# Early keys in fp32 on the SyncE queue with a ScalarE cast, a halved output copy, and new engine orders, in a fused attention and expert kernel

## The chip, the cores and the metric

The kernel runs on one NeuronCore of one Trainium2 chip. The metric is the device time of one execution in microseconds (us); smaller is better. A trace also gives the span from the first to the last instruction, about 1.8 us shorter than that time. Engines: PE (TensorE matmuls), PEld (its weight loads), ACT (ScalarE), DVE (VectorE), POOL (GpSimd), SP (SyncE, which only issues DMAs here). "Granted clock" is TensorE's share of full speed.

Most executions of one kernel agree within a per cent; now and then one takes 2 to 3% longer, as one of the first three of the kernel before did (175.25 us). Those count as slow and are left out of every ratio and median below.

## The reference

Shortened and rewritten. Eight batches, eight heads, 576 positions, head width 64. Keys and values are averaged over groups of eight positions, attention runs on the 72 pooled keys, and its output `x` (8 x 576 x 512) goes through four attention experts with causal masks, of which two are picked for each position.

```python
def reference(q, k, v, w_gate, wq, wk, wv, wo):        # shortened
    k_p = k.reshape(B, H, 72, 8, 64).mean(axis=3)       # pooling
    v_p = v.reshape(B, H, 72, 8, 64).mean(axis=3)
    attn = softmax(q @ k_p.T / 8.0)
    x = (attn @ v_p).transpose(0, 2, 1, 3).reshape(B, 576, 512)
    logits = x @ w_gate                                 # 4 experts, top 2, weights by softmax
    for e in range(4):
        a = softmax(causal(x @ wq[e] @ (x @ wk[e]).T / 8.0))
        out += gate[e] * (a @ (x @ wv[e]) @ wo[e])
    return out                                          # 8 x 576 x 512, fp32
```

## The kernel before

One long list of tokens gives PE, ACT, DVE and POOL their orders. A token is a step, its batch after the colon, its PSUM bank after `@`, and a final `d` if DVE, not ACT, does the copy. Each engine runs its own steps strictly in the list's order. POOL issues the loads and also applies the causal masks.

```python
def load(b, nm, c):          # L_q, L_k, L_v: fp32 in HBM, bf16 in SBUF: the DMA casts on its way
    if nm == "q":
        dst = qraws[b % NRAW][:, c, :, :]
        ...
    nc.gpsimd.dma_start(out=dst, in_=src)

def warm_up(n, bank):        # Hn: n matmuls on nothing, to bring the clock up and keep it up
    for _ in range(n):
        nc.tensor.matmul(out=psum[:, bank, :], lhsT=warm[:, 0:128], rhs=warm[:], start=True, stop=True)

def am(b, ep, ti):           # a00 ... a12: causal mask on POOL, after ACT's exp of the same scores
    ...
            nc.gpsimd.affine_select(out=blk, in_=blk, ...)

def y(b, bank, dve, c):      # last step of a tile: copy out of PSUM, then DMA to HBM on SyncE
    ofin = ofp.tile([128, DM], FP32, name="ofin", tag="ofin")     # 8 buffers in turn
    copy(dve, ofin[:], psum[:, bank, :])
    if c == 4:
        for h in range(2):   # two half tiles, two DMAs
            nc.sync.dma_start(out=out[b - 1 + h, MAIN:S, :], in_=ofin[64 * h : 64 * h + 64, :])
    else:
        nc.sync.dma_start(out=out[b, 128 * c : 128 * c + 128, :], in_=ofin[:])

SEQ = """ I:0 L_k0:0 L_k1:0 L_k2:0 J:0 L_q0:0 K:0 L_q1:0 L_q2:0 L_q3:0 L_q4:0 L_q5:0 H19:0@0
          PK:0@0 L_v0:0 kc:0d L_v1:0 H3:0@1 KT:0@0 ...
          ... Y4:7@5 y1:7 Y2:7@6 y2:7d y4:7d """
```

`PK` pools the keys, `KT` and `Q` transpose keys and queries, `E` are the first scores, `P` the expert projections, `S`, `B`, `T`, `Y` the expert scores, values, transposes and output.

The softmax here doesn't subtract the row's maximum and nothing guards it: scores larger than these inputs give would overflow.

Of the kernel before, what the change touches and what calls it, by code (L numbers as in the profile page):

```python
# [8 lines left out]
FP32 = mybir.dt.float32  # L9
# [12 lines left out]
def kernel(  # L22
# [33 lines left out]
    KR = 96  # L56
# [52 lines left out]
    def load(b, nm, c):  # L109
        if nm == "q":  # L110
            dst = qraws[b % NRAW][:, c, :, :]
            src = q[b, :, KR * c : KR * (c + 1), :].rearrange("h p d -> p h d")
        else:
            raw, T = (kraws, k) if nm == "k" else (vraws, v)
            dst = raw[b % NRAW][:, c, :, :, :].rearrange("p h t d -> p h (t d)")
            src = T[b, :, 2 * KR * c : 2 * KR * (c + 1), :].rearrange("h (p t) d -> p h (t d)", t=2)
        nc.gpsimd.dma_start(out=dst, in_=src)  # L117

# [376 lines left out]
    def y(b, bank, dve, c):  # L495
        ofin = ofp.tile([128, DM], FP32, name="ofin", tag="ofin")
        copy(dve, ofin[:], psum[:, bank, :])
        if c == 4:
            for h in range(2):
                nc.sync.dma_start(out=out[b - 1 + h, MAIN:S, :], in_=ofin[64 * h : 64 * h + 64, :])  # L500
        else:
            nc.sync.dma_start(out=out[b, 128 * c : 128 * c + 128, :], in_=ofin[:])
# [7 lines left out]
        I:0 L_k0:0 L_k1:0 L_k2:0 J:0 L_q0:0 K:0 L_q1:0 L_q2:0 L_q3:0 L_q4:0 L_q5:0 H19:0@0  # L510
        PK:0@0 L_v0:0 kc:0d L_v1:0 H3:0@1 KT:0@0 L_v2:0 kt:0 L_k0:1 L_k1:1 H8:0@1 Q0:0@0 Q2:0@1
        r0:0 Q3:0@2 L_k2:1 Q1:0@3 r3:0d E0:0@4 r1:0 r2:0d L_q0:1 E3:0@6 M:0 e0:0 E4:0@2 E2:0@0
        L_q1:1 e3:0 E1:0@4 L_q2:1 e1:0 L_q3:1 PV:0@6 L_q4:1 vc:0d e4:0 H1:0@7 D0:0@4 e2:0 L_q5:1
        H1:0@5 D2:0@5 O01:0@6 O00:0@7 d0:0 W1:0 H1:0@2 O11:0@0 O10:0@1 x0:0 O20:0@2 D1:0@4 d2:0
        d1:0 o00:0 W0:0 H1:0@3 PK:1@3 o01:0 kc:1 W3:0 x1:0 H3:0@5 KT:1@3 W2:0 kt:1 o11:0 x2:0
        o10:0 L_v0:1 L_v1:1 H9:0@4 Q1:1@3 Q0:1@1 L_v2:1 r1:1d Q2:1@0 r0:1 Q3:1@6 L_k0:2 E1:1@4
        r3:1d c2:0 c3:0d H1:0@3 E0:1@6 L_k1:2 e1:1 r2:1d P_k0:0@3 o20:0 E3:1@4 L_k2:2 p_k0:0
        E4:1@0 P_k1:0@2 c0:0 L_q0:2 c1:0 P_q0:0@3 e4:1 c4:0d L_q1:2 e3:1 P_q1:0@0 p_k1:0d e0:1
        V2:0@1 p_q0:0d L_q2:2 V0:0@2 p_q1:0d E2:1@4 S00:0@6 v0:0d e2:1 V1:0@3 L_q3:2 v2:0d
        P_t0:0@2 v1:0d s00:0 D1:1@4 PV:1@3 L_q4:2 d1:1 V3:0@5 vc:1d a00:0 D0:1@6 x1:1 v3:0d  # L520
        L_q5:2 O10:1@3 d0:1 O11:1@4 o10:1 D2:1@5 S10:0@0 p_t0:0 O01:1@6 x0:1 o11:1 L_v0:2
        O00:1@7 S02:0@2 s10:0 o01:1 PK:2@4 L_v1:2 o00:1 d2:1 x2:1 S01:0@0 s02:0 g1:0 L_v2:2
        V3:1@5 kc:2d P_q0:1@7 g2:0 L_k0:3 s01:0 v3:1d g3:0 g4:0 L_k1:3 Q1:2@6 p_q0:1 Q0:2@0
        r1:2d KT:2@1 g0:0 L_k2:3 V1:1@5 r0:2d Q2:2@4 kt:2d L_q0:3 Q3:2@0 v1:1d r2:2 V2:1@1 r3:2d
        E0:2@6 L_q1:3 g5:0 v2:1 E2:2@4 E3:2@2 e0:2 P_k0:1@1 L_q2:3 e3:2 a02:0 P_q1:1@0 p_k0:1d
        L_q3:3 e2:2 E1:2@2 p_q1:1d S03:0@6 PV:2@1 a10:0 e1:2 L_q4:3 O20:1@4 D1:2@0 o20:1 V0:1@5
        vc:2d d1:2 L_q5:3 P_t0:1@4 s03:0 v0:1d V4:1@2 L_v0:3 x1:2 p_t0:1d D0:2@3 g6:0 O01:2@5
        L_v1:3 d0:2 O00:2@4 O11:2@6 PK:3@7 x0:2 o11:2 W4:0 O10:2@3 S02:1@0 v4:1 o01:2 P_k1:1@6
        kc:3 L_v2:3 o00:2 g0:1 s02:1 L_k0:4 KT:3@7 o10:2 Q3:3@5 Q0:3@4 L_k1:4 r3:3 Q1:3@2 g1:1
        Q2:3@3 g2:1 r0:3d r1:3 V2:2@0 a01:0 kt:3d P_q0:2@1 p_k1:1 g3:1 L_k2:4 g4:1 r2:3d g5:1  # L530
        v2:2d S12:0@6 a03:0 p_q0:2 S11:0@2 g6:1 L_q0:4 g7:0 S00:1@4 g8:0 s12:0 V3:2@0 g9:0
        L_q1:4 P_k1:2@1 v3:2d s11:0 g7:1 L_q2:4 g8:1 B00:0@0 s00:1 V1:2@6 a11:0 bz00:0 bg00:0
        P_k0:2@7 a12:0 b00:0 p_k1:2 v1:2d L_q3:4 E4:2@4 p_k0:2d E1:3@2 e4:2 E2:3@0 V0:2@6 a00:1
        g9:1 e2:3 L_q4:4 B10:0@7 v0:2d B11:0@4 bz10:0 L_q5:4 e1:3 bg10:0 D2:2@6 PV:3@5 bz11:0
        bg11:0 L_v0:4 S01:1@0 d2:2 vc:3d S10:1@2 x2:2 B01:0@6 s01:1 L_v1:4 b10:0 P_q1:2@5 bz01:0
        L_v2:4 s10:1 bg01:0 b01:0 E3:3@0 b11:0 L_k0:5 S12:1@6 p_q1:2d e3:3 S11:1@2 PK:4@4 a01:1
        g1:2 a02:1 T1:0@5 s12:1 kc:4d T0:0@0 Q1:4@1 L_k1:5 t1:0d D1:3@4 s11:1 r1:4d E0:3@6
        L_k2:5 t0:0d O20:2@5 Q0:4@1 e0:3 o20:2 Y0:0@0 L_q0:5 r0:4d Q2:4@5 g2:2 E4:3@2 d1:3
        L_q1:5 r2:4d S03:1@6 Y3:0@1 e4:3 y0:0d P_t0:2@5 L_q2:5 s03:1 y3:0d D0:3@4 x1:3 D2:3@6
        O11:3@7 a11:1 p_t0:2d O10:3@0 d2:3 O01:3@1 d0:3 o11:3 a12:1 O00:3@6 O20:3@5 S02:2@2 x0:3  # L540
        o10:3 a03:1 KT:4@7 s02:2 a10:1 B01:1@4 o00:3 L_q3:5 B00:1@0 bz01:1 g3:2 kt:4 B10:1@6
        o01:3 L_q4:5 x2:3 B11:1@2 g0:2 bz00:1 bg01:1 bz10:1 Q3:4@1 o20:3 L_q5:5 P_k0:3@7 bz11:1
        r3:4d bg11:1 L_v0:5 bg00:1 bg10:1 b00:1 P_k1:3@5 p_k0:3 b01:1 L_v1:5 b11:1 P_q1:3@7
        p_k1:3 b10:1 L_v2:5 E2:4@4 p_q1:3d L_k0:6 S00:2@0 e2:4 S01:2@2 V0:3@6 g4:2 L_k1:6 V2:3@7
        s00:2 v0:3d V3:3@4 L_k2:6 v2:3d V1:3@5 s01:2 L_q0:6 V4:3@0 v1:3d Q1:5@1 v3:3 v4:3d
        L_q1:6 E3:4@6 S10:2@2 g1:3 e3:4 T0:1@0 r1:5d a01:2 Q2:5@4 t0:1d a00:2 P_q0:3@5 s10:2
        g5:2 L_q2:6 r2:5d g6:2 g2:3 Q3:5@0 p_q0:3d a02:2 E1:4@6 E4:4@2 PK:5@1 e1:4 g3:3 r3:5d
        L_q3:6 PV:4@5 g4:3 g7:2 g8:2 D1:4@0 e4:4 L_q4:6 vc:4d B00:2@6 d1:4 S03:2@2 g9:2 L_q5:6
        bz00:2 E0:4@4 kc:5d s03:2 Y2:0@7 e0:4 L_v0:6 bg00:2 P_t0:3@2 y2:0d T1:1@3 x1:4 L_v1:6
        KT:5@1 b00:2 D0:4@0 g0:3 D2:4@7 t1:1d O00:4@4 d0:4 a03:2 O11:4@6 kt:5d O20:4@5 L_v2:6  # L550
        O10:4@3 g5:3 p_t0:3 O01:4@1 g6:3 x0:4 o10:4 PV:5@0 L_k0:7 Y1:0@2 o11:4 vc:5 Y4:1@3
        L_k1:7 d2:4 o00:4 B01:2@0 x2:4 y1:0 o20:4 a10:2 S12:2@6 y4:1 o01:4 L_k2:7 S11:2@4
        P_t0:4@2 s12:2 g7:3 bz01:2 g8:3 L_q0:7 P_q0:4@1 g9:3 bg01:2 s11:2 b01:2 L_q1:7 p_t0:4d
        Q0:5@6 Y3:1@0 p_q0:4d r0:5 a12:2 V2:4@4 y3:1d S10:3@2 a11:2 S00:3@6 v2:4d s10:3 S02:3@0
        L_q2:7 V0:4@5 V3:4@4 L_q3:7 s02:3 v0:4d Q0:6@2 P_k0:4@3 L_q4:7 r0:6d s00:3 v3:4d L_q5:7
        B10:2@2 E3:5@0 p_k0:4 bz10:2 E2:5@6 L_v0:7 bg10:2 e3:5 E0:5@4 b10:2 B11:2@3 a00:3 Y2:1@2
        e2:5 L_v1:7 bz11:2 bg11:2 V1:4@0 y2:1d P_q1:4@1 a02:3 e0:5 b11:2 v1:4d a10:3 E4:5@2
        E1:5@6 p_q1:4d e4:5 S01:3@4 Y0:1@0 e1:5 T1:2@1 y0:1d T0:2@2 P_k1:4@3 s01:3 t1:2d t0:2d
        S03:3@0 S12:3@6 p_k1:4d a01:3 s03:3 S11:3@4 Q3:6@2 s11:3 Y0:2@3 Y3:2@0 y0:2d s12:3
        D0:5@1 a11:3 D1:5@4 y3:2d PK:6@3 d0:5 O20:5@5 g1:4 a12:3 D2:5@6 O10:5@7 kc:6d d2:5  # L560
        O00:5@0 d1:5 O11:5@1 a03:3 r3:6d O01:5@6 x2:5 Y1:1@3 L_v2:7 x1:5 o20:5 Q1:6@2 B10:3@4
        o11:5 r1:6 V4:5@5 o10:5 x0:5 B11:3@2 y1:1 bz10:3 Y2:2@1 o00:5 v4:5 Q2:6@7 bg10:3 KT:6@3
        g0:4 bz11:3 y2:2 o01:5 B01:3@0 B00:3@5 kt:6 r2:6d Q3:7@1 bz01:3 V3:5@3 bg01:3 bz00:3
        g2:4 r3:7 b01:3 V0:5@7 bg11:3 bg00:3 b10:3 Q0:7@6 v0:5 V2:5@1 b11:3 v3:5 P_q0:5@4 r0:7d
        v2:5d b00:3 T1:3@6 p_q0:5 V1:5@7 t1:3d S01:4@2 g3:4 v1:5d E3:6@4 s01:4 S02:4@0 g1:5
        P_k0:5@7 g4:4 g2:5 g3:5 s02:4 a01:4 T0:3@6 p_k0:5d P_k1:5@2 e3:6 a02:4 g4:5 t0:3d
        S00:4@0 p_k1:5d E2:6@6 g0:5 s00:4 E0:6@4 Y3:3@3 P_q1:5@2 e2:6 y3:3d a00:4 S10:4@0 e0:6
        p_q1:5d E1:6@6 PV:6@3 g5:5 g5:4 g6:5 s10:4 g6:4 D1:6@2 vc:6d Y1:2@4 Q2:7@5 g7:4 d1:6
        y1:2d Y1:3@3 a10:4 e1:6 P_t0:5@0 r2:7d PK:7@2 y1:3d x1:6 S03:4@4 g7:5 g8:4 D0:6@1 kc:7d
        s03:4 O10:6@3 O01:6@6 d0:6 a03:4 o10:6 O00:6@7 O11:6@2 p_t0:5 S11:4@4 x0:6 o11:6 S12:4@0  # L570
        B01:4@3 s11:4 o00:6 Y0:3@2 o01:6 s12:4 B00:4@7 a11:4 Q1:7@4 g9:4 g8:5 bz00:4 V1:6@6
        r1:7d y0:3 a12:4 S00:5@0 bg00:4 v1:6 b00:4 E4:6@4 V2:6@2 s00:5 g9:5 bz01:4 KT:7@7
        P_q1:6@6 v2:6d e4:6 kt:7d a00:5 bg01:4 S12:5@0 b01:4 E3:7@4 p_q1:6d S02:5@2 e3:7 B11:4@7
        P_q0:6@6 bz11:4 s02:5 bg11:4 b11:4 B10:4@4 p_q0:6d s12:5 V0:6@5 a02:5 bz10:4 V3:6@2
# [80 lines left out]
```

## Time and profile before

| kernel before | |
|---|---|
| time, three runs | 170.39, 170.50, 175.25 us (the last slow) |
| span of the profiled run, granted clock | 168.5 us, 1.000 |
| PE busy, of it warm-ups | 156.5 us, 12.8 us (45) |
| start of the last part of the first pooling, of the first scores, of the first projection | 8.38, 13.22, 25.60 us |
| last matmul, last landing, end of the span | 162.96, 167.61, 168.53 us |

The profile's page of the kernel before, busy time and the chain of waits (the chain that ended last, followed back):

```profile
PE 156.5 (93%) x2075; PEld 91.5 (54%) x2103; DVE 123.3 (73%) x395; ACT 135.2 (80%) x240; POOL 105.7 (63%) x178
...
PE 66%; ACT 10%; POOL 10%; DMA 4%; DVE 4%; issue 3%; DVEq 1%; POOLq 0%
```

PE bounds the kernel; only its idle times, its warm-ups and the two ends are to be had. The timeline of PE at the start (start, duration, engine, line, what; in brackets the idle time before and what ended it):

```profile
1.26 5.96 PE L172 MATMUL psum<-warm 128*128 128x512 bf16 x19 [1.26 <-DVE onesd L146]
...
8.38 0.59 PE L178 MATMUL psum<-kraw_71,poolk 96*32 96x512 bf16 x4 [0.85 <-DMA kraw_71<-in_k_dram]
...
12.27 0.98 PE L182 MATMUL psum<-ident,qraw_68 96*128 96x96 bf16 x19 [0.23 <-DMA qraw_68<-in_q_dram]
13.22 0.42 PE L178 MATMUL psum<-qT_83,kpT_79 64*96 64x512 bf16 x2
...
25.60 0.81 PE L178 MATMUL psum<-xT_95,wkp_122 128*128 128x512 bf16 x3 [0.28 <-ACT wkp_122 L175]
```

Pooling waits for keys, the query transposes wait for queries, which POOL issues from 4.05 us, behind the keys. POOL issues the key loads first, from 1.35 us, and then the queries, from 4.05 us.

```profile
1.35 2.42 POOL L117 DMA_DIRECT2D kraw_71<-in_k_dram  x3 [0.84 <-POOLq L639]
...
4.05 4.59 POOL L117 DMA_DIRECT2D qraw_68<-in_q_dram  x6
...
59.97 0.78 POOL L117 DMA_DIRECT2D kraw_73<-in_k_dram  x1
60.74 1.16 POOL L438 TENSOR_SCALAR_AFFINE_SELECT etb_98<-etb_98 128x256 bf16<-128x256 bf16 x3
61.86 1.53 POOL L117 DMA_DIRECT2D kraw_73<-in_k_dram  x2
```

The windows view, 60 to 76 us (window, its length, busy time of PE, PEld, DVE, ACT and POOL with their counts, clock, DMA share, GB/s); PE is nearly full:

```profile
60.00:76.00 16.00, 15.82 (x261) 10.37 (x262) 14.29 (x45) 13.37 (x24) 15.76 (x25) 1.00 1.80 180
```

And the timeline of the end: two copies in a row on DVE, then two issues on SyncE:

```profile
162.96 0.38 PE L178 MATMUL psum<-wop,oT_112 128*128 128x512 bf16 x1
163.43 1.29 DVE L175 COPY ofin<-psum 128x512 f32<-128x512 f32 x2 [0.66 <-PE psum L178]
164.75 1.11 SPq L500 DMA_DIRECT2D out_dram<-ofin  x2
```

### The profile page before, as it was taken

The page shows a single profiled execution, that of the slowest core. Times are in us where ns is not written, and L with a number is a line of the kernel's source. Part 1 is how long each engine was busy: PE and PEld are TensorE (multiplying, and loading weights), DVE is VectorE, ACT ScalarE, POOL GpSimd, SP SyncE. Part 2 cuts the span into 40 slices and gives each one's busy share as a digit, 9 for nine tenths or more (in the row PEclk, how much of TensorE's full clock was granted, in tenths as well). Part 3 has the DMA queues.
Part 4 walks back from the last instruction along what each step waited for, and adds up shares of the span by engine and source line. Part 5 has one row for each costly group of instructions (what it writes and reads, how often), then busy time and mean ns, then how long its engine had stood idle before and what let it go on. Part 6 is the DMA issues. An engine that isn't in the chain of part 4 may idle for free.

```text
span 168.5 us, 5320 instructions
## 1 busy us (share of the span) xinstructions
PE 156.5 (93%) x2075; PEld 91.5 (54%) x2103; DVE 123.3 (73%) x395; ACT 135.2 (80%) x240; POOL 105.7 (63%) x178
## 2 busy tenths in 40 slices
PE   7797999999999999999999999999999999999960
PEld 2343354546565646765666557744665556756720
DVE  1115465686787899969996789979977896699940
ACT  3019949897999999678998999699988989898750
POOL 7999996799997999999998624021222021435100
PEclk9999999999999999999999999999999999999999
DMA  2999999999999999999999997401310043007576
GB/s 23 157 158 174 163 172 180 176 160 176 164 180 182 144 137 175 230 163 176 160 211 220 207 216 169 138 0 64 128 62 4 0 175 141 4 20 229 197 294 202
DMA packets 84201, 24.99 MB, mean 148 GB/s; under 512 B 79312, under 2 KB 79568, under 8 KB 84176
## 3 DMA queue, kind: packets, MB, share of 16 engines
q0 software_dynamic: 78928, 15.21, 107.5%
q1 hardware_dynamic: 5248, 9.44, 15.9%
q8 instruction: 16, 0.26, 0.6%
q14 instruction: 9, 0.07, 0.1%
HBM read 30.42 MB, written 9.44 MB: 236 GB/s over the span
## 4 chain that ended last, share of the span: by engine, by line
PE 66%; ACT 10%; POOL 10%; DMA 4%; DVE 4%; issue 3%; DVEq 1%; POOLq 0%
PE psum L178 59%; PE psum L182 7%; DMA wst_k<-in_moe_wk_dram 4%; POOL qraw_69 L117 3%; POOL qraw_68 L117 3%; ACT etb_97 L421 2%; ACT eta_92 L261 2%; ACT rza_94 L282 2%; ACT rza_94 L286 1%; POOL kraw_71 L117 1%; POOL kraw_72 L117 1%; POOL vraw_74 L117 1%; ACT etb_98 L421 1%; ACT eta_92 L255 1%; DVEq L650 1%
## 5 line engine op out<-in xcount | busy, mean ns | idle before, releaser
L421 ACT ACTIVATE etb_98<-psum 128x1024 bf16<-128x1024 f32 x24 | 23.7, 1026 | 2.4 <-PE psum L178 1.8
L438 POOL TENSOR_SCALAR_AFFINE_SELECT etb_97<-etb_97 128x256 bf16<-128x256 bf16 x32 | 12.5, 408 | 20.8 <-ACT etb_97 L421 20.6
L438 POOL TENSOR_SCALAR_AFFINE_SELECT etb_98<-etb_98 128x256 bf16<-128x256 bf16 x32 | 12.6, 409 | 19.7 <-ACT etb_98 L421 19.6
L421 ACT ACTIVATE etb_97<-psum 128x1024 bf16<-128x1024 f32 x24 | 23.9, 1028 | 0.7 <-PE psum L178 0.5
L261 ACT ACTIVATE eta_91<-psum 96x1024 bf16<-96x1024 f32 x16 | 15.8, 1028 | 1.3 <-PE psum L178 1.3
L261 ACT ACTIVATE eta_92<-psum 96x1024 bf16<-96x1024 f32 x16 | 15.7, 1021 | 1.3 <-PE psum L178 1.2
L175 DVE COPY ofin<-psum 128x512 f32<-128x512 f32 x20 | 13.4, 685 | 4.0 <-PE psum L178 3.9
L117 POOL DMA_DIRECT2D qraw_69<-in_q_dram x18 | 13.8, 773 | 0.4 <-issue 0.3
L172 PE MATMUL psum<-warm 128*128 128x512 bf16 x45 | 12.8, 426 | 1.3 <-DVE onesd L146 1.3
L117 POOL DMA_DIRECT2D qraw_68<-in_q_dram x18 | 13.8, 772 | 0.0
L178 PE MATMUL psum<-wvg,xT_95 128*128 128x260 bf16 x72 | 10.6, 275 | 0.2
L175 ACT COPY ofin<-psum 128x512 f32<-128x512 f32 x16 | 9.2, 588 | 1.8 <-PE psum L178 1.8
L178 PEld LDWEIGHTS <-etb_97 128*128 128x128 bf16 x240 | 8.6, 97 | 3.1 <-issue 1.6
L178 PE MATMUL psum<-wvg,xT_96 128*128 128x260 bf16 x72 | 10.1, 275 | 0.0
L175 DVE CAST qk_99<-psum 128x512 bf16<-128x512 f32 (+1 forms) x14 | 8.9, 647 | 1.5 <-PE psum L178 1.4
L117 POOL DMA_DIRECT2D qraw_70<-in_q_dram x12 | 9.2, 769 | 1.1 <-DMA vraw_75<-in_v_dram 1.0
L172 PEld LDWEIGHTS <-warm 128*128 128x128 bf16 x47 | 4.7, 107 | 8.7 <-issue 4.6
L175 DVE CAST qk_100<-psum 128x512 bf16<-128x512 f32 (+1 forms) x11 | 7.0, 640 | 3.2 <-PE psum L178 3.0
L178 PE MATMUL psum<-qk_99 64*128 64x64 bf16 (+4 forms) x96 | 9.1, 278 | 0.1
L178 PEld LDWEIGHTS <-etb_98 128*128 128x128 bf16 x240 | 8.5, 97 | 0.8
L178 PE MATMUL psum<-qk_100 64*128 64x64 bf16 (+4 forms) x96 | 8.7, 276 | 0.0
L175 DVE CAST vaug_102<-psum 128x256 bf16<-128x256 f32 x13 | 5.5, 424 | 3.7 <-PE psum L178 3.7
(194 smaller groups left out, 445.8 us busy)
## 6 DMA issues: line engine op xcount, KB each, us to landing
out_dram<-ofin SPq DMA_DIRECT2D x32, 256.0 KB, 2.2
kraw_71<-in_k_dram POOLq DMA_DIRECT2D x9, 192.0 KB, 6.0
qraw_68<-in_q_dram POOLq DMA_DIRECT2D x18, 96.0 KB, 4.9
vraw_74<-in_v_dram POOLq DMA_DIRECT2D x9, 192.0 KB, 5.3
kraw_72<-in_k_dram POOLq DMA_DIRECT2D x9, 192.0 KB, 7.4
qraw_69<-in_q_dram POOLq DMA_DIRECT2D x18, 96.0 KB, 6.6
vraw_75<-in_v_dram POOLq DMA_DIRECT2D x9, 192.0 KB, 6.5
kraw_73<-in_k_dram POOLq DMA_DIRECT2D x6, 192.0 KB, 7.1
```

Of the source, the lines that this page charges most:

```text
L117: nc.gpsimd.dma_start(out=dst, in_=src)
L172: nc.tensor.matmul(out=psum[:, bank, :], lhsT=warm[:, 0:128], rhs=warm[:], start=True, stop=True)
L175: (nc.vector.tensor_copy if dve else nc.scalar.copy)(out=out, in_=in_)
L178: nc.tensor.matmul(out=out, lhsT=lhsT, rhs=rhs, start=start, stop=stop)
L182: nc.tensor.transpose(out=out, in_=in_, identity=ident[0:n, 0:n])
L255: nc.scalar.activation(out=eta[:, :, hh, MAIN:S], in_=psum[0:KR, bank + hh, 0 : NHP * TAIL].rearrange("p (a n) -> p a n", a=NHP), func=EXP ...
L261: nc.scalar.activation(out=eta[:, hp, :, 0:MAIN], in_=psum[0:KR, bank : bank + 2, :], func=EXP, scale=ATT_EXP_SCALE,)
L282: nc.scalar.activation(out=part(rzas[b % 2], g), in_=z, func=LN)
L286: nc.scalar.activation(out=rz, in_=rz, func=EXP, scale=-1.0)
L421: nc.scalar.activation(out=et[:, ep, :, eo : eo + n], in_=psum[:, bank : bank + 2, 0:n], func=EXP, scale=MOE_EXP_SCALE,)
L438: nc.gpsimd.affine_select(out=blk, in_=blk, pattern=[[0, 2], [1, 128]], compare_op=ISGE, fill=0.0, base=0, channel_multiplier=-1,)
L650: with _tile.TileContext(nc) as tc:
```

## The change

The intent: start loading earlier, by giving the first three key loads to SyncE, whose queue is idle then. A SyncE DMA here does not cast, so the keys come in fp32 into a buffer that is not in use yet, and ACT, idle at the start, casts them. The end: the output tile `y3` of the last batch is copied in halves by DVE and ACT, and the tile with two DMAs goes to ACT. All four orders were planned anew around this.

```diff
+    early = etbs[0][0:KR].rearrange("p a b n -> p (a b n)").bitcast(FP32)[:, 0 : 3 * H * 2 * D]
+    ...                                                  # early_part(c): its part c, 1024 elements a row
+    def load_early(c):                                   # token X
+        src = k[0, :, 2 * KR * c : 2 * KR * (c + 1), :].rearrange("h (p t) d -> p h (t d)", t=2)
+        nc.sync.dma_start(out=early_part(c), in_=src)
+    def cast_early(c):                                   # token kx
+        nc.scalar.copy(out=kraws[0][:, c, :, :, :].rearrange("p h t d -> p h (t d)"), in_=early_part(c))
-    def y(b, bank, dve, c):
+    def y(b, bank, dve, c, half=None):                   # tokens ya (ACT), yb (DVE)
+        ofin = at[b, "ofin", c] if (b, "ofin", c) in at else ofp.tile([128, DM], FP32, ...)
+        if half is not None:
+            cols = slice(256 * half, 256 * half + 256)
+            copy(half == 1, ofin[:, cols], psum[:, bank, cols])
+            ...                                          # DMA after the second half
 SEQ = """
-        I:0 L_k0:0 L_k1:0 L_k2:0 J:0 L_q0:0 K:0 L_q1:0 L_q2:0 L_q3:0 L_q4:0 L_q5:0 H19:0@0
-        PK:0@0 L_v0:0 kc:0d L_v1:0 H3:0@1 KT:0@0 L_v2:0 kt:0 L_k0:1 L_k1:1 H8:0@1 Q0:0@0 Q2:0@1
+        I:0 X0:0 X1:0 J:0 X2:0 kx0:0 kx2:0 L_q0:0 L_q1:0 K:0 kx1:0 H20:0@0 PK:0@0 kc:0d H3:0@1
+        KT:0@0 kt:0d L_q2:0 L_q3:0 L_q4:0 L_q5:0 H5:0@1 Q0:0@0 r0:0d Q1:0@1 r1:0d Q2:0@2 Q3:0@3
  ...  (80 lines of tokens replaced by 80 others)
+        ... x0:1 a03:0 O20:1@0 ... L_k2:2 ... L_q5:2 ...
+        ... L_v2:4 a03:1 a01:1 ... L_k0:5 L_k1:5 ... L_k2:5 ...
-        bg11:7 y2:6 Y3:6@7 b11:7 t0:7 T1:7@6 y3:6 t1:7d Y3:7@6 Y0:7@7 y3:7 Y1:7@4 y0:7d Y4:7@5
-        y1:7 Y2:7@6 y2:7d y4:7d
+        bg10:7 b10:7 T1:7@5 t1:7d Y3:7@5 yb3:7d y3:6 ya3:7 Y4:7@4 Y0:7@2 y0:7 y4:7 Y1:7@5 y1:7
+        Y2:7@3 y2:7d
```

## The prediction

> **What bounds the kernel now.** The busy table gives PE 156.5 of 168.5 us, ACT 135.2, DVE 123.3. In the chain of waits PE holds 66%, nearly unbroken from 38 to 163 us. The windows of 4 us show PE idle mostly at the two ends: it starts at 1.25 us, is idle 2.8 us between then and 28 us, 0.6 us between 160 and 163.3 us, and has no work in the last 5.2 us. 12.8 us of its busy time are 45 warm-up matmuls, nearly all before 24 us. So the start is bound by loading: the chain there is POOL issuing DMAs without a gap from 1.35 to 18.06 us (0.77 us each), then the load of the k weights, landing at 24.7 us. DMA carries nothing before 3 us, then a flat 150 to 180 GB/s of bf16 (twice that is read, because these DMAs cast), so throughput limits the loads too. First keys land at 8.38 us, first queries at 12.27, first scores run at 13.2.
>
> **What the change moves.** Start: the first three key loads leave POOL (3 x 0.77 = 2.3 us of issue; queries can be issued from 1.4 us instead of 4.1). SyncE issues them at about 0.9 us. The Trainium skill, "DMA: Bandwidth & Descriptors", section "Latency and other measured facts", gives HWDGE a first byte after about 0.6 us against 1 us for SWDGE; no run here yet shows this for a load. I estimate that transfers start 1.0 to 1.3 us earlier. The bytes read from HBM remain, so queries land 1.2 to 1.5 us earlier (10.8 to 11.1 us), not 2.3. Added: three ScalarE casts of 96x1024; ACT instructions of that size take 1.02 us in the trace, so 3 us, while ACT was idle from 2.1 to 10.1 us: hidden, except that the last cast delays the first pooling by 1 us after its landing. Keys have slack before the queries. The weights move with POOL's queue, to about 22.9 us.
>
> The new order has 47 warm-ups, as before, so PE can only gain what it was idle: at most 2.5 us at the start. I expect 1.4 us.
>
> End: now the last copies are two in a row on DVE (163.43 to 164.72 us), followed by two DMA issues (1.11 us). In the new order the tile with two issues goes to ACT, and one DVE copy (0.68 us) with one issue (0.33 us) is last. The halved tile is not the last one written; halving frees its PSUM bank 0.25 us sooner. I expect 1.4 us less after the last matmul.
>
> Middle: PE work is the same; the reorder is worth 0, give or take 0.8 us. POOL and DMA finish loading 2 us earlier, at about 107 us, which is worth nothing there.
>
> **Sum.** 170.4 (fast runs) - 1.4 - 1.4 = 167.6 us; range 166.0 to 169.3. Faster by over 2% (under 167.0): 0.33; within 2%: 0.65; slower: 0.02.
>
> **What would show each step.** POOL's first load of queries is issued near 1.4 us; DMA share rises at 2.2 us instead of 3.3; queries land near 11 us, scores start near 11.7, the weights land near 23; PE idle plus warm-up before 28 us falls by 1.4 us; from the last matmul to the end is 3.8 us instead of 5.2; ACT busy rises by 3 us, PE busy stays within 1 us.
>
> **What would make it wrong.** fp32 on SyncE is slow (512-byte packets, 768 per DMA) or shares the engines badly with the queries, so that pooling waits beyond the queries: then the start gives nothing, 169 us. If those packets move faster than casting ones, the start gives 2.5 us. The new order could create waits in the middle, where ACT (31 to 38 us) and DVE (148 to 154 us) appear in the chain, or remove them.

## The result, and the profile after

The kernel after took 172.19 us (median of four fast runs, 171.92 to 173.15), the kernel before 170.50 in the fast runs of the same rounds (170.39, 170.50, 170.63). The ratio is 1.0109, 95% interval 1.0059 to 1.0158. All ratios here are the mean time of one kernel's fast runs over that of the other's of the same rounds, so not quite the ratio of the medians. It is 1.1% slower, where 1.6% faster was predicted, and it lies outside the range.

The page of the kernel after, busy time, queues and chain:

```profile
PE 156.6 (92%) x2078; PEld 91.3 (54%) x2103; DVE 120.8 (71%) x388; ACT 139.3 (82%) x251; POOL 103.0 (60%) x175
...
q1 hardware_dynamic: 7600, 10.62, 19.1%
...
PE 56%; DMA 16%; POOL 13%; issue 5%; DVE 4%; ACT 2%; SPq 1%; DVEq 0%; POOLq 0%
...
etb_97<-in_k_dram SPq DMA_DIRECT2D x3, 384.0 KB, 5.5
```

PE is busy as long as before, ACT 4 us longer. SyncE's queue (q1) has 7600 packets in place of 5248; each of its three key loads of 384 KB takes 5.5 us (median) from issue to landing. What grew is DMA in the chain: 4% before, 16% now (by line: 7.4% loads of queries, 3.9% the early keys, 3.8% batch 5's keys). PE's timeline at the start:

```profile
1.26 7.33 PE L185 MATMUL psum<-warm 128*128 128x512 bf16 x20 [1.26 <-DVE onesd L159]
8.52 0.39 PE L191 MATMUL psum<-kraw_71,poolk 96*32 96x512 bf16 x1
10.54 0.61 PE L191 MATMUL psum<-kraw_71,poolk 96*32 96x512 bf16 x5 [1.63 <-ACT kraw_71 L130]
...
12.13 1.24 PE L185 MATMUL psum<-warm 128*128 128x512 bf16 x5
13.21 1.19 PE L195 MATMUL psum<-ident,qraw_68 96*128 96x96 bf16 x24
...
14.94 0.42 PE L191 MATMUL psum<-qT_86,kpT_79 64*96 64x512 bf16 x2 [0.33 <-DVE qT_86 L188]
...
26.04 0.81 PE L191 MATMUL psum<-xT_95,wkp_122 128*128 128x512 bf16 x3 [0.16 <-issue]
```

The last part of the pooling starts at 10.54 us, 2.2 us later than before, and what ends its wait is a cast. The query transposes wait for no query now: the sixth had landed at 11.83 us, so the five warm-ups ahead of them (1.08 us in the chain of waits, from 12.29 us) fill no wait any more. ACT's and POOL's timelines of the start, POOL's of 24 to 32 and of 60 to 66 us, and PE's at 71 us:

```profile
5.03 1.04 ACT L130 CAST kraw_71<-etb_97 96x1024 bf16<-96x1024 f32 x1 [2.94 <-DMA etb_97<-in_k_dram]
8.50 1.99 ACT L130 CAST kraw_71<-etb_97 96x1024 bf16<-96x1024 f32 x2 [2.42 <-DMA etb_97<-in_k_dram]
...
1.45 4.71 POOL L117 DMA_DIRECT2D qraw_68<-in_q_dram  x6 [0.31 <-issue]
...
29.62 0.42 POOL L443 TENSOR_SCALAR_AFFINE_SELECT etb_97<-etb_97 64x256 bf16<-64x256 bf16 x1 [4.15 <-ACT etb_97 L428]
...
62.35 0.42 POOL L443 TENSOR_SCALAR_AFFINE_SELECT etb_98<-etb_98 64x256 bf16<-64x256 bf16 x1 [1.33 <-ACT etb_98 L428]
...
63.34 1.54 POOL L117 DMA_DIRECT2D kraw_73<-in_k_dram  x2
...
65.59 0.77 POOL L117 DMA_DIRECT2D kraw_73<-in_k_dram  x1
...
71.34 0.38 PE L191 MATMUL psum<-kraw_73,poolk 96*32 96x512 bf16 x1 [0.94 <-DMA kraw_73<-in_k_dram]
72.17 0.59 PE L191 MATMUL psum<-kraw_73,poolk 96*32 96x512 bf16 x4 [0.45 <-DMA kraw_73<-in_k_dram]
```

The first cast takes 1.04 us; two more follow back to back from 8.50 us. The Trainium skill, "ScalarE: Activation LUTs", section "What ACT_TABLE_LOAD costs", gives 186 ns plus 0.833 ns for each element of a row, 1.04 us for 1024: this trace agrees, for a copy too. Later, masks stand in POOL's order ahead of loads: POOL stands still for 4.15 us before 29.62 us, and batch 5's keys are issued at 63.34 to 66.36 us in place of 59.97 to 63.39. PE then waits for exactly these keys. The windows view, 60 to 76 us, shows what it costs PE, 14.22 us busy in place of 15.82:

```profile
60.00:76.00 16.00, 14.22 (x188) 7.90 (x189) 10.94 (x27) 13.26 (x24) 13.22 (x21) 1.00 1.75 192
```

And the end:

```profile
162.81 0.43 DVE L188 COPY ofin<-psum 128x256 f32<-128x256 f32 x1 [0.68 <-DMA out_dram<-ofin]
...
163.32 1.92 ACT L188 COPY ofin<-psum 128x256 f32<-128x256 f32 x4 [1.32 <-issue]
...
164.39 0.38 PE L191 MATMUL psum<-wop,oT_112 128*128 128x512 bf16 x1
164.78 1.12 SPq L521 DMA_DIRECT2D out_dram<-ofin  x2
164.80 0.69 DVE L188 COPY ofin<-psum 128x512 f32<-128x512 f32 x1 [1.56 <-PE psum L191]
165.99 1.02 SPq L523 DMA_DIRECT2D out_dram<-ofin  x2
```

The halves do not run side by side: DVE's half waits for an output buffer and ends at 163.24 us, ACT's starts 0.08 us later, after ACT had been idle for 1.32 us. The two halves write one tile; that this is why the second waits is likely, not shown.

Where the span's 1.9 us (170.4 less 168.5) came from, read from the two traces: the last matmul starts 1.43 us later (164.39 less 162.96), and from there to the end it takes 0.48 us longer:

| from the last matmul's start | before | after |
|---|---|---|
| to the end of the last DMA issue on SyncE | 2.90 | 2.62 |
| from there to the last landing | 1.75 | 2.16 |
| from there to the end of SyncE's closing waits | 0.08 | 0.43 |
| from there to the end of the span | 0.84 | 0.84 |

The packets of the start, read from the trace: how many began in each half microsecond on the SyncE queue (S: fp32 keys, 512 bytes) and on the POOL queue (P: casting loads of keys, then queries); the last column is the run `d1_keys_alone`, below, in which nothing else was loaded until the keys had landed.

```
from us   before P     after S    after P    d1 S     mean time of a packet on S, after
 2.0           0           90          0      101      34 ns
 2.5           6          260          0      235      28 ns
 3.0          79          339          0      337      27 ns
 3.5         154          255          0      278      38 ns
 4.0         351          227          0      222      43 ns
 4.5         355          209          0      220      46 ns
 5.0         351          236          0      230      40 ns
 5.5         321          193         10      231      47 ns
 6.0         256          199         61      236      43 ns
 6.5         299          181        123      191      41 ns
 7.0         470          114        318       37      38 ns
 7.5         546           30        539        0      37 ns
 8.0         602            1        607        0
```

The SyncE loads do start early: issued from 0.81 us, first packet at 1.86 us, against 1.35 and 2.95 us for POOL's keys before. So issue to first packet is 1.05 and 1.60 us here. The Trainium skill ("DMA: Bandwidth & Descriptors", "Latency and other measured facts") has 0.6 against 1 us; both figures are longer here, and SyncE's is again the shorter, by 0.55 us in place of 0.4. But the keys land at 5.01, 6.76 and 8.47 us, against 5.33, 6.49 and 8.34 us before: 1.1 us of head start, and the last one lands 0.13 us later. And the queries, which POOL issued 2.6 us earlier, hardly move while the keys do: the sixth lands at 11.83 us, before at 12.23.

### The profile page after: what moved, and what is told of

Same layout as the page of the kernel before. It is cut to its first block, busy times and chain, and to the rows that moved or that the text cites. A ratio compares the mean times of both kernels' runs of the same rounds, so it can differ in the third digit from the quotient of the medians.

```text
span 170.4 us, 5321 instructions
## 1 busy us (share of the span) xinstructions
PE 156.6 (92%) x2078; PEld 91.3 (54%) x2103; DVE 120.8 (71%) x388; ACT 139.3 (82%) x251; POOL 103.0 (60%) x175
## 4 chain that ended last, share of the span: by engine, by line
PE 56%; DMA 16%; POOL 13%; issue 5%; DVE 4%; ACT 2%; SPq 1%; DVEq 0%; POOLq 0%
PE psum L191 48%; DMA qraw_68<-in_q_dram 7%; PE psum L195 6%; DMA etb_97<-in_k_dram 4%; DMA kraw_73<-in_k_dram 4%; POOL qraw_68 L117 4%; POOL qraw_70 L117 3%; PE psum L185 3%; POOL etb_97 L451 2%; POOL kraw_71 L117 2%; ACT kraw_71 L130 1%; DVE ofin L188 1%; POOL kraw_73 L117 1%; POOL vraw_76 L117 1%; DMA out_dram<-ofin 1%
## 5 line engine op out<-in xcount | busy, mean ns | idle before, releaser
L434 ACT ACTIVATE etb_97<-psum 128x1024 bf16<-128x1024 f32 x24 | 24.0, 1025 | 1.7 <-PE psum L191 1.7
L434 ACT ACTIVATE etb_98<-psum 128x1024 bf16<-128x1024 f32 x24 | 24.3, 1032 | 0.5 <-PE psum L191 0.5
L274 ACT ACTIVATE eta_92<-psum 96x1024 bf16<-96x1024 f32 x16 | 16.0, 1024 | 1.4 <-PE psum L191 1.4
L188 DVE COPY ofin<-psum 128x512 f32<-128x512 f32 (+1 forms) x18 | 11.9, 670 | 6.4 <-PE psum L191 5.7
L185 PE MATMUL psum<-warm 128*128 128x512 bf16 x45 | 13.9, 456 | 1.4 <-DVE onesd L159 1.3
L117 POOL DMA_DIRECT2D qraw_68<-in_q_dram x18 | 13.9, 779 | 0.3 <-issue 0.3
L188 ACT COPY ofin<-psum 128x512 f32<-128x512 f32 (+1 forms) x19 | 10.7, 578 | 3.2 <-PE psum L191 1.9
L188 DVE CAST qk_99<-psum 128x512 bf16<-128x512 f32 (+1 forms) x13 | 8.4, 648 | 4.0 <-PE psum L191 3.7
L188 DVE CAST qk_100<-psum 128x512 bf16<-128x512 f32 (+1 forms) x14 | 9.1, 650 | 2.4 <-PE psum L191 2.2
L191 PE MATMUL psum<-wvg,xT_95 128*128 128x260 bf16 x72 | 10.4, 275 | 0.1
L191 PE MATMUL psum<-wvg,xT_96 128*128 128x260 bf16 x72 | 10.4, 275 | 0.0
L191 PE MATMUL psum<-qk_100 64*128 64x64 bf16 (+4 forms) x96 | 9.4, 276 | 0.0
L191 PE MATMUL psum<-qk_99 64*128 64x64 bf16 (+4 forms) x96 | 8.9, 277 | 0.0
L117 POOL DMA_DIRECT2D vraw_74<-in_v_dram x9 | 6.9, 771 | 1.7 <-DMA qraw_68<-in_q_dram 1.3
```

The lines of the kernel that those rows point to most:

```text
L188: (nc.vector.tensor_copy if dve else nc.scalar.copy)(out=out, in_=in_)
L191: nc.tensor.matmul(out=out, lhsT=lhsT, rhs=rhs, start=start, stop=stop)
L274: nc.scalar.activation(out=eta[:, hp, :, 0:MAIN], in_=psum[0:KR, bank : bank + 2, :], func=EXP, scale=ATT_EXP_SCALE,)
L434: nc.scalar.activation(out=et[:, ep, :, eo : eo + n], in_=psum[:, bank : bank + 2, 0:n], func=EXP, scale=MOE_EXP_SCALE,)
```

## The experiments

All kernels computed the reference's result. Medians are in us, ratios are to the kernel before in the same rounds. The time of the kernel before was 170.4 to 170.8 in all of them. Edits are given as changes of tokens.

### First four: which part of the change costs

`a1_keys_pool`: the kernel after, with the early keys on POOL as before.

```diff
-  I:0 X0:0 X1:0 J:0 X2:0 kx0:0 kx2:0 L_q0:0 L_q1:0 K:0 kx1:0 H20:0@0
+  I:0 L_k0:0 L_k1:0 L_k2:0 J:0 L_q0:0 L_q1:0 K:0 H20:0@0
```

> The kernel after, with one part undone: the first three key loads are issued by POOL again, as casting loads, before the iota, and the three ScalarE casts are gone. The new order and the halved copy stay. Theory START (the early fp32 load is what costs: it holds the DMA engines until 7.8 us and its casts put the first pooling at 10.5 us instead of 8.4): pooling back at about 8.4 us, scores near 13.2 us, the time falls by 1 us or more, to 171.2 or less. Rival PLAN (the new fixed order costs, mostly because POOL meets masks ahead of loads and PE then starves at 48 to 76 us): the start recovers but the wait of POOL near 25 to 29 us and the PE wait near 70 us remain, and the time stays within 0.5 us of 172.2.

Measured: 171.28, ratio 1.0049 (0.9997 to 1.0101). Scores start at 13.84 us, 1.1 us earlier than in the kernel after. POOL still stands still 3.22 us before the mask at 29.49 us, and ACT's half copy still waits 1.55 us. So the new order has costs of its own, whatever the early keys do. (The interval overlaps the kernel after's; `e2_loads_first` and `e3_loads_sync` below make the same comparison more sharply.)

`a2_whole`: the kernel after, with the copy whole.

```diff
-  Y3:7@5 yb3:7d y3:6 ya3:7 Y4:7@4
+  Y3:7@5 y3:6 y3:7 Y4:7@4
```

> The kernel after, with the halved copy made whole again (one ScalarE copy, after the other output copy of ScalarE). Theory TAIL (the two halves run one after the other, the second starting 0.08 us after the first has ended, and the buffer is claimed one output earlier, so it waits for a DMA): ACT no longer sits idle 1.3 us before 163.3 us, the last matmul ends 0.6 to 1.0 us earlier, the time is 171.3 to 171.6. Rival (the tail is bound by SyncE's issues and the last matmuls alone): no change, 172.2.

Measured: 173.44 (four fast runs of six), ratio 1.0144 (1.0088 to 1.0200). It can't be used for the copy: in the profiled run PE idled 3.52 us before the pooling and its clock was halved from 11.38 to 14.79 us. `a5_whole` repeats the test without that. The two kernels have the same start, so this is chance: here the clock rose to full at 4.56 us and the first warm-ups were done at 7.36 us; in the kernel after's trace it rose at 7.04 us, the warm-ups lasted until 8.59 us, and PE idled only 1.63 us. One of the kernel after's four runs, 173.15 us with a mean clock of 0.982 where the others have 0.989 to 0.991, may have met the same; without it its ratio would be 1.0093.

`b1_early`: the kernel before, with only the early keys changed.

```diff
-  I:0 L_k0:0 L_k1:0 L_k2:0 J:0 L_q0:0
+  I:0 X0:0 X1:0 J:0 X2:0 kx0:0 kx2:0 kx1:0 L_q0:0
```

> The kernel before, with only the early keys put in (fp32 on SyncE, three ScalarE casts); order and end as before. START: pooling moves from 8.4 to about 10.5 us, scores from 13.2 to about 14.5, and the time rises by 0.5 to 1.3 us, to 171 to 171.8. Rival, the prediction's (POOL's 2.3 us of freed issue makes the whole load stream earlier): weights land 1 to 2 us earlier than 24.7 us and the time falls to about 169.

Measured: 174.52, ratio 1.0214 (1.0164 to 1.0263): the early keys alone cost more than the whole change. PE's timeline:

```profile
1.26 5.84 PE L185 MATMUL psum<-warm 128*128 128x512 bf16 x19 [1.26 <-DVE onesd L159]
7.03 0.39 PE L191 MATMUL psum<-kraw,poolk 96*32 96x512 bf16 x1
10.92 0.71 PE L191 MATMUL psum<-kraw,poolk 96*32 96x512 bf16 x5 [3.50 <-ACT kraw L130]
```

From 11.29 us the granted clock is 0.5 for 3.41 us, and scores start at 16.79 us. The Trainium skill, "TensorE: Matmul & The Clock Gate", Part 1, names a window of 3413 ns after which an idle PE is throttled to half: this trace agrees in the sizes, 3.50 us idle and 3.41 us at half clock, though the clock fell only 0.37 us after PE had begun to work again.

`b2_tail`: the kernel before, with the end as the prediction understood it: the tile with two DMAs first, one copy and one issue last.

```diff
-  Y4:7@5 y1:7 Y2:7@6 y2:7d y4:7d
+  Y4:7@5 y1:7 y4:7d Y2:7@6 y2:7
```

> The kernel before, with only the last two copies changed: the tile with two output DMAs is copied first (DVE), the other one last and on ScalarE. By the prediction's step for the end: the last SyncE issue ends at about 165.1 us instead of 165.86, so the time falls by 0.7 us, to 169.8. Rival (output bandwidth or the landing of the last data bounds the end, not the order of copies): within 0.2 us of 170.5.

Measured: 170.29, ratio 0.9981 (0.9946 to 1.0016), no gain shown, though the interval would still allow the 0.4% that was expected. The last copy ends at 164.69 us, but SyncE is busy with the two issues from 164.42 to 165.54 us, and the last issue ends at 166.17 us, 2.52 us after the last matmul's start in place of 2.90. It lands 1.93 us later in place of 1.75, so 0.2 us of the hoped 0.7 us is left in the trace. The order of the copies matters less than the queue of issues behind them.

### Next four: clock, masks, copy, and a smaller dose

`b3_early_warm`: `b1_early` with 16 more warm-ups, so that PE does not idle (`H19` becomes `H35`).

> The run b1_early (the kernel before plus early keys; 174.5 us) with 16 more warm-up matmuls in the first block (35 for 19), which cover the time that PE waits for the casts (7.4 to 10.9 us). Theory CLOCK (a PE that stays idle for about 3.5 us loses half its clock for the next 3.41 us, 11.3 to 14.7 us in b1_early, and that, not the late keys alone, makes most of the 4 us): granted clock 1.0 between 5 us and the end, scores about 1.5 us earlier than 16.8 us, the time falls by 1.5 to 2 us, to about 172.7. Rival (all of the loss is the lateness of keys and queries; clock is a side effect): within 0.4 us of 174.5, or worse by the added matmuls.

Measured: 172.88, ratio 1.0136 (1.0107 to 1.0166), clock 1.0 from 5.25 us on, scores at 15.38 us. So of `b1_early`'s loss of about 3.7 us, some 1.3 us was the clock (0.0078 of 170.7), and about 2.3 us came with the late keys. That is not all lateness of data: the sixth query had landed at 11.97 us, yet the eight warm-ups that stand behind the pooling in the old order kept PE until 14.40 us (1.73 us). No run took them out.

`a4_masks`: `a1_keys_pool` with the first late mask moved behind the loads that it held up.

```diff
-  x0:1 a03:0 O20:1@0 ... L_k2:2 ... L_q5:2 v3:1d
+  x0:1 O20:1@0 ... L_k2:2 ... L_q5:2 a03:0 v3:1d
```

> The run a1_keys_pool (new order, keys loaded by POOL as before; 171.3 us) with one token moved: the first mask that POOL meets, for which it waited 3.2 us near 26 to 29 us, now stands behind the key and query loads of the third batch instead of ahead of them. Theory PLAN (loads that stand behind a mask in POOL's queue come late, and PE starves at 50 and at 64 to 76 us): POOL is not idle near 26 us, the loads run about 3 us earlier up to about 60 us, PE idle between 60 and 100 us falls from 1.5 us to under 0.8 us, and the time falls by 0.5 to 1 us, to about 170.5. Rival (the load stream has slack by then, or a later mask holds it up again): POOL's wait goes but the time stays within 0.2 us of 171.3.

Measured: 170.98, ratio 1.0014 (0.9977 to 1.0051). POOL's long wait is gone and PE is busy 31.94 us from 28 to 60 us. But PE still waits for batch 5's keys at 70 us, since another mask stands in front of those at 61.57 us.

`a5_whole`: `a1_keys_pool` with the copy whole.

> The run a1_keys_pool with the halved copy made whole on ScalarE, so that the tail is judged without the early keys, which made the granted clock differ from run to run in a2_whole. Theory TAIL: ACT's wait of 1.5 us before 163 us goes, the copy starts when its matmul ends (162.0), the matmuls behind it start about 0.5 to 0.9 us earlier and the time falls by as much, to 170.4 to 170.8. Rival (ACT then holds a 0.58 us copy more in a row of four and SyncE issues end as late as before): within 0.2 us of 171.3.

Measured: 170.44, ratio 0.9987 (0.9944 to 1.0029), 0.6% under `a1_keys_pool`'s ratio, with intervals that overlap. ACT's timeline at the end, where the wait of 1.55 us is gone:

```profile
162.38 0.59 ACT L188 COPY ofin<-psum 128x512 f32<-128x512 f32 x1 [0.76 <-PE psum L191]
163.24 1.56 ACT L188 COPY ofin<-psum 128x512 f32<-128x512 f32 x3 [0.28 <-PE psum L191]
```

But the two traces end alike: the last matmul starts 0.37 us earlier (163.69 against 164.06 us), and from there to the last landing takes 0.35 us more (5.04 against 4.69). So the wait of ACT is explained, a gain from the whole copy is not shown.

`b4_split`: the kernel before, with only the first third of the keys on SyncE, the others on POOL.

```diff
-  I:0 L_k0:0 L_k1:0 L_k2:0 J:0 L_q0:0
+  I:0 X0:0 L_k1:0 L_k2:0 J:0 kx0:0 L_q0:0
```

> The kernel before with only one of the first three key loads as fp32 on SyncE with a cast; the two others stay on POOL as casting loads, issued first. In b1_early and after, the fp32 packets flow at about 320 per 0.5 us only until 4 us, then at about 215, and no query packet moves until about 6 us. Theory OVERLAP (what hurts is that 2304 fp32 packets hold the DMA engines until 7.8 us, while one load of 768 would be through at about 4 us, before POOL's packets come): first pooling at 6.5 to 7.5 us instead of 8.4, queries land 0.8 to 1.2 us earlier than 12.27, the time falls by 0.3 to 1 us, to 169.4 to 170.1. Rival (any fp32 load beside POOL's loads slows both, and the cast delays pooling): pooling no earlier than 8.4 us, time 170.4 or more.

Measured: 170.48, ratio 0.9988 (0.9965 to 1.0012). The start is what was hoped for: scores at 12.47 us (13.22 before), first projection at 24.36 us (25.60), last matmul at 162.22 us (162.96), last landing at 166.89 us (167.61). But SyncE's closing waits end 0.98 us after the landing in place of 0.08, which takes the gain back. So an earlier start is worth about 0.7 us, and something at the end hides it.

### Then: the closing waits, everything together, keys without company

`b5_lanes`: `b4_split`, and the first seven output DMAs cut in two, so that SyncE issues 48 DMAs in place of 41.

```diff
+            for h in range(2) if 4 * b + c < 7 else [None]:
+                rows = slice(0, 128) if h is None else slice(64 * h, 64 * h + 64)
+                nc.sync.dma_start(out=out[b, 128 * c + rows.start : 128 * c + rows.stop, :], in_=ofin[rows, :])
```

> The run b4_split (old order, one early fp32 key load: 170.5 us although its last output landed 0.7 us earlier than before's) with one change far from the end: seven early output DMAs are issued in two halves each, so SyncE issues 48 DMAs in place of 41. The program ends with SyncE checking its DMA semaphores one by one, in a fixed order of eight; the semaphores go round with every DMA. With 40 (before) the last one issued is checked last, 0.08 us passed between the last landing and the end of the checks; with 41 it is checked first, and the other checks came after it, 0.98 us. Theory CHECKS: with 48 the time between last landing and end of the checks is 0.1 us again and the time falls by 0.6 to 0.9 us, to 169.6 to 169.9. Rival (the end was late for another reason, for example a slow landing): no change, 170.5, or worse by the added issues.

Measured: 170.13 (one slow run of six left out), ratio 0.9950 (0.9912 to 0.9987), a little less gain than expected. The closing waits end 0.08 us after the landing again. Over all traces, the time from last landing to the end of these waits goes with the number of DMAs that SyncE issued: 40 (kernel before, `a1_keys_pool`): 0.08 and 0.11 us; 43 (kernel after, `b1_early`): 0.43 and 0.41; 41: 0.98; 48: 0.08. In the trace SyncE goes at the end through a list of semaphores, one after another, about 0.07 us each. Its DMAs use eight of them in turn. In the kernel before, the last DMA's semaphore is the last of the eight in that list; in the kernel after five more follow it, and with 41 DMAs seven more, one of which took 0.45 us for a reason that the trace does not show.

`c1_best`: the new order with split keys, first mask moved, whole copy and 48 DMAs.

> The new order with everything mended that the runs so far found: one early fp32 key load instead of three (two on POOL, first), the first mask behind the loads, the output copy whole, 48 SyncE DMAs. If the losses are separate, the gains add up: a1_keys_pool 171.3, less 0.6 (mask), less 0.8 (whole copy), less 1 (split keys): 168.9 to 169.8, faster than before by 0.5 to 1%. If the new order is itself no better than the old one, it ends no earlier than b5_lanes.

Measured: 170.73, ratio 0.9999 (0.9960 to 1.0038). A miss: the gains did not add. Scores start at 12.61 us, but PE was busy only 37.64 us from 60 to 100 us, waiting for loads.

`a8_repaired`: the kernel after with its early keys, but the first late mask moved, the copy whole, and 34 warm-ups in front in place of 20 to guard the clock.

> The kernel after with all three early fp32 key loads kept, but mended otherwise: mask behind the loads, output copy whole, and 14 more warm-up matmuls in the first block so that PE is never idle for 3.5 us. Theory START (three early fp32 loads cost by themselves, through late keys and queries): granted clock full from 7 us on in every run, time 171.2 to 171.8, so 1 us or more over what the same order does with keys on POOL (a4_masks 171.0, a5_whole 170.4). Rival (masks, copy and clock are all of the loss): 170.2 or less.

Measured: 171.85, ratio 1.0059 (1.0018 to 1.0100). The rival (170.2 or less) falls: the early keys cost by themselves.

`d1_keys_alone` (one look): the kernel after with POOL's loads held back by 22 fillers on POOL, and 34 warm-ups, to see the fp32 keys alone.

> The kernel after, with POOL held up by 22 dummy iotas (about 5.5 us) before its first query load, and 14 more warm-ups: a measurement of the three fp32 key loads with nothing else on the DMA engines; slow on purpose. In after the fp32 packets go at 320 per 0.5 us until 4 us and at 211 afterwards, before any query packet is recorded. Theory CONTENTION (POOL's waiting casting loads take the engines' time): 320 per 0.5 us to the end, last key packet at about 5.7 us instead of 7.8. Rival (SyncE's fp32 loads slow down by themselves, for example from the second DMA on): still about 211 after 4 us and the last packet at about 7.5 us.

Measured: 174.91 (one run; the time is of no interest). In the packet table above the keys move no faster alone: up to 337 packets in a half microsecond at first, then 220 to 236, and the last lands at 7.9 us in place of 8.5. So the queries cost the keys some 0.5 us at the end; for the rest the fp32 loads are slow by themselves. The turn comes at about the end of the first of the three DMAs, whose 768th and last packet begins at 3.6 us here and in the kernel after (in `b1_early` some 0.3 us after it). Why the second and third run slower (42 ns for a packet on average in this run, the first 28 ns) stays open.

### Last five: do the costs add up

`e1_pool_masks_whole`: `a4_masks` and `a5_whole` together.

> The kernel after with the early keys back on POOL, the first mask behind the loads, and the last copy whole: the two repairs that gave 170.98 and 170.44 singly (kernels before of 170.7), together. If start, mask and tail are separate costs: 170.0 to 170.4, PE at 28 to 60 us about 31.9 us busy, at 60 to 76 still only 14.8 to 15.2. If the gains overlap (the 60 to 76 us stall eats them, as in the run with everything together): 170.4 to 170.8.

Measured: 170.44, ratio 0.9993 (0.9964 to 1.0023): no better than `a5_whole` alone. The first mask, with the longest wait of all, was worth nothing that these runs resolve: moving it took the ratio down by 0.0035 from `a1_keys_pool` to `a4_masks`, and up by 0.0006 from `a5_whole` to here. The whole copy, 0.0062 in the first pair, is 0.0021 in this one (`a4_masks` to here).

`e2_loads_first`: the same, and batch 5's key loads moved ahead of the mask that POOL waits for at 61.4 us.

```diff
-  L_v2:4 a03:1 a01:1 ... L_k0:5 L_k1:5 ... L_k2:5
+  L_v2:4 L_k0:5 L_k1:5 L_k2:5 a03:1 a01:1 ...
```

> The same, and the three key loads of batch 5 moved ahead of the mask on which POOL waits at about 61.6 us. Theory (a mask ahead of loads in POOL's order delays them, and PE starves for them at 68 to 72 us): key loads issued by about 62 us, PE busy at 60 to 76 us up from about 15.0 to 15.5 or more, and the time 0.3 to 0.8 us below the run before this one. Rival (the loads are late for bandwidth, or the stall only moves to the next load): PE at 60 to 76 us or 76 to 100 us loses the same again, time unchanged within 0.2 us.

Measured: 169.93, ratio 0.9946 (0.9917 to 0.9975): three tokens are worth about 0.8 us (0.0047 of 170.6; the intervals just overlap). POOL's timeline, in which the mask waits for nothing any more:

```profile
60.47 2.33 POOL L117 DMA_DIRECT2D kraw<-in_k_dram  x3
62.85 0.42 POOL L443 TENSOR_SCALAR_AFFINE_SELECT etb<-etb 64x256 bf16<-64x256 bf16 x1
```

The windows view, 60 to 76 us, has PE at 15.43 us busy, against 14.99 in `e1_pool_masks_whole`:

```profile
60.00:76.00 16.00, 15.43 (x203) 8.76 (x203) 11.78 (x31) 14.42 (x27) 15.14 (x25) 1.00 1.85 207
```

`e3_loads_sync`: `e2_loads_first` with the three early fp32 keys and 34 warm-ups, as in `a8_repaired`.

> The same as the second, but with the early keys in fp32 on SyncE and cast by ScalarE as in the kernel after, and the 61 warm-up matmuls' worth of clock guard (34 in the first group). Compared in the same rounds this isolates the start. Theory (early fp32 keys cost about 1.2 us, since queries land no earlier and the casts delay the pooling): 1.0 to 1.5 us over the second run. Rival (the start costs nothing once the rest is repaired, the loss is the plan's): within 0.4 us of it.

Measured: 170.81, ratio 1.0022 (0.9986 to 1.0058), 1.3 us over `e2_loads_first` in the same rounds (0.0076 of 170.6). Some 0.3 us of it is the clock guard: the last cast ended at 11.05 us, and the 34 warm-ups let the pooling begin at 11.36 us.

`e4_cast_order`: `e3_loads_sync` with the casts in the order of landing, and 28 warm-ups in place of 34.

```diff
-  kx0:0 kx2:0 L_q0:0 L_q1:0 K:0 kx1:0 H34:0@0 PK:0@0
+  kx0:0 kx1:0 kx2:0 L_q0:0 L_q1:0 K:0 H28:0@0 PK:0@0
```

> The run that kept the fp32 early keys with the order repaired (170.81, ratio 1.0022), with the casts in the order in which the keys land: in the kernel after, the cast of the third part is ahead of the second's, though the second landed at 6.76 us and the third at 8.47 us; 28 warm-ups ahead of the pooling in place of 34. If the cast order is part of the cost of the early keys: one cast, not two, follows the last landing, the pooling starts 0.8 to 1.2 us earlier (11.4 to about 10.3 us), scores 15.8 to about 14.8 us, and the time falls by 0.4 to 1.0 us. Rival (queries landing late set the start, not the pooling): scores no earlier than 15.4 us and the time unchanged within 0.2 us.

Measured: 169.97 (five fast runs of six; the sixth, 171.72, is just past the limit, and with it the ratio would be 0.9983), ratio 0.9969 (0.9928 to 1.0010). ACT's timeline:

```profile
5.16 1.04 ACT L130 CAST kraw<-etb 96x1024 bf16<-96x1024 f32 x1 [3.08 <-DMA etb<-in_k_dram]
6.68 1.04 ACT L130 CAST kraw<-etb 96x1024 bf16<-96x1024 f32 x1 [0.47 <-DMA etb<-in_k_dram]
9.22 1.04 ACT L130 CAST kraw<-etb 96x1024 bf16<-96x1024 f32 x1 [1.50 <-DMA etb<-in_k_dram]
```

One cast, not two, follows the last landing. Pooling starts at 10.17 us in place of 11.36 and scores at 14.69 us in place of 15.81, as the theory said; the rival, that late queries set the start, falls. The time fell by 0.8 us by the medians and 0.9 us by the ratios (0.0053 of 170.6); the intervals overlap. Of the 1.19 us by which the pooling starts earlier, the casts account for 0.79 us (the last one ends at 10.26 in place of 11.05 us) and the six warm-ups fewer for the rest.

`e5_split_loads`: `e2_loads_first` with the split keys of `b4_split` and 48 DMAs on SyncE.

> The best order so far (the new order with two masks behind the loads, whole last copy: 169.93) with only the first third of the early keys in fp32 on SyncE, and 48 DMAs on SyncE in place of 41 for the cheap end. If gains add: ratio to before 0.988 to 0.992 (168.6 to 169.2 us), scores at about 12.6 us. Rival (a start 1 us earlier is eaten later by waits for loads and masks, as when everything was put together before): 169.7 to 170.2, no faster than 169.93 by over 0.2 us.

Measured: 169.55, ratio 0.9927 (0.9900 to 0.9953), the fastest of all, 0.7% under the kernel before and by the ratios 1.8% under the kernel after. It differs from `c1_best` (0.9999) only in where three loads stand. The time lies within neither expectation: better than the rival's, short of full addition.

## Why the prediction was wrong

The way from the kernel after to the fastest one, each step a change of ratio, taken as us of 170.6. Each ratio is to the kernel before in the same rounds; the steps between are smaller than the intervals in part, so the sizes are estimates.

| step | ratio | us |
|---|---|---|
| kernel after | 1.0109 | |
| first mask moved, copy whole, clock guarded (`a8_repaired`) | 1.0059 | -0.9 |
| batch 5's keys ahead of a mask (`e3_loads_sync`) | 1.0022 | -0.6 |
| casts in the order of landing (`e4_cast_order`) | 0.9969 | -0.9 |
| early keys back on POOL (`e2_loads_first`) | 0.9946 | -0.4 |
| one third of them on SyncE, 48 DMAs (`e5_split_loads`) | 0.9927 | -0.3 |

**What bounds the kernel.** Right: PE is busy for as long in both (156.5 and 156.6 us), and of its idle and warm-up time neither end gave any back.

**"I estimate that transfers start 1.0 to 1.3 us earlier."** Right: 1.86 against 2.95 us. A little luck was in it: the parts that it named, 0.45 us by the issue and 0.4 us by the first byte, make 0.85 us, and both were larger (0.54 and 0.55 us).

**"so queries land 1.2 to 1.5 us earlier ... I expect 1.4 us."** This step failed. The sixth query landed 0.4 us earlier (11.83 against 12.23). The prediction carried the head start through the whole row of loads. But the second and third fp32 load run at two thirds of the pace of the first, alone or not (`d1_keys_alone`), and until 7 us few query packets move beside them. Even the 0.4 us was not used: pooling had become what PE waits for, and five warm-ups stood behind it.

**"hidden, except that the last cast delays the first pooling by 1 us after its landing. Keys have slack before the queries."** This step failed too. The cast's size was right (1.04 us), but two of them followed the last landing, because the plan casts the third part before the second, which had been there since 6.76 us. Pooling went from 8.38 to 10.54 us, past the slack, and scores from 13.22 to 14.94; 1.08 us of the way between passed in those five warm-ups, which no run took out. I had the order `kx0 kx2 kx1` in the diff before me and did not set it against the order of the loads. By the first projection the delay was down to 0.44 us, at the price of less work done in between: real work of PE before 28 us, without the warm-ups, was 10.4 us in place of 11.1 (24.32 - 13.9 and 23.93 - 12.8).

**"Middle: ... the reorder is worth 0, give or take 0.8 us."** The size was off. From 60 to 76 us PE lost 1.6 us of work, waiting for keys that POOL issued some 3 us late, since a mask stood ahead of them. Moving those loads alone gave back about 0.8 us (`e2_loads_first`), and with split keys 1.2 us (`c1_best` to `e5_split_loads`, 0.0072 of 170.6, intervals apart). The prediction named new waits in the middle as a risk, but looked for them at ACT and DVE, and counted POOL's earlier finish as "worth nothing": it took POOL's total for its order.

**"End: ... I expect 1.4 us less after the last matmul."** This step failed: it is 0.48 us more. The estimate followed one tile, the last copy and its issue. SyncE takes issues one at a time, so the two of the tile before still hold up the last: the issues end only 0.28 us sooner after the last matmul (2.62 against 2.90), and `b2_tail`, which is that step alone, brought the landing 0.2 us closer. Landing took 0.41 us longer after its issue. That goes with the new order: 2.14 to 2.36 us in all its 13 traces, 1.75 to 1.84 us in the five with the old end. In these the last issue is half a tile, in the new order a whole one, as in `b2_tail` (1.93 us); that the size is the cause is not shown. The closing waits took 0.35 us more, with 43 DMAs in place of 40.

**"The halved tile is not the last one written; halving frees its PSUM bank 0.25 us sooner."** It did not: ACT's half started only after DVE's had ended, and ACT stood still for 1.32 us with other copies behind it. Yet the halves cost little: with a whole copy the ratio is 0.6% lower in one pair and 0.2% in the other, neither clear of noise, and the trace of `a5_whole` ends as that of `a1_keys_pool`.

**"fp32 on SyncE is slow (512-byte packets, 768 per DMA)".** This was given as the way to be wrong, with 169 us as the outcome. It is what happened at the start, but the outcome was worse, because the start did not merely give nothing, and neither middle nor end gave what was expected.

## What to carry to other kernels

Before crediting a faster first transfer, follow the loads to the last one that the consumer needs, and lay the order of their conversions beside the order of landing: one swapped cast put the end of the last cast off by 0.79 us, about what the head start was worth (0.7 us). On an engine that issues loads and also computes, read its order line by line for steps that wait ahead of loads; three loads moved ahead of one mask gave 0.5%, while removing the longest visible wait gave nothing that could be resolved. Where an order holds fillers for a wait, move them when the wait moves. And change an end as a queue, not as a last item: count the issues behind each other and the waits that close the program.

## What the Trainium skill lacked or had wrong

- "DMA: Bandwidth & Descriptors", "Queues, rings and completion order", says that each DMA engine takes turns between the queues that have work. In the start of the kernel after, 193 key packets of SyncE's queue began in the half microsecond from 5.5 us and 10 of POOL's query packets, though POOL had issued its first query at 1.45 us and its first packet came 4.3 us later. With no keys of SyncE in flight the first packet comes 1.60 us (kernel before) or 1.59 us (`d1_keys_alone`) after POOL's issue, beside one such load 2.07 us (`b4_split`). So the delay goes with the keys in flight; no run here shows whether the engines or POOL's preparation of the loads held the queries back.
- The same page, "Latency and other measured facts": 0.6 us and 1 us to the first byte. Here the first packets began 1.05 us after the start of the issue on SyncE and 1.60 us on POOL.
- No page tells that of three equal fp32 loads in a row on one queue the first moves a packet in 28 ns and the others in 42 ns (means in `d1_keys_alone`, with nothing else loading).
- No page has the closing waits on SyncE inside the program: 0.08 to 0.11 us after the last landing with 40 or 48 DMAs issued by SyncE, 0.41 to 0.43 us with 43, 0.98 us with 41.
- "ScalarE: Activation LUTs" has its formula for ACTIVATE; a copy with a cast, 1024 fp32 elements to bf16, fits it too (1.04 us).
